# Top-32 attention followed by a gated feed-forward: token blocks of 256 in the feed-forward, other buffer counts, and the split first in GpSimd's order

## The chip, the cores and the metric

The kernel runs on one core of a Trainium2 chip. The core has five engines that each work through their own instructions in order: TensorE (matrix multiply; PE in the profile, PEld its weight loads), VectorE (DVE), ScalarE (ACT), GpSimd (POOL) and SyncE (SP, here only a queue of DMA issues). They meet at semaphores. The metric is the time of one execution on the device, in microseconds (us). The kernel before takes 1498.96 us, the median of three runs (1487.91, 1498.96, 1499.81).

## The reference

Attention for 8 batches x 8 heads, 576 tokens of 64 dimensions each. In every row of scores only the 32 largest survive. The result, 4608 tokens x 512, goes through a feed-forward of width 2048 with the activation h cos(h):

```python
scores = scale * np.matmul(q, k.transpose(0, 1, 3, 2))       # scale = 1/8
kth = np.partition(scores, -32, axis=-1)[..., -32:-31]
scores = np.where(scores >= kth, scores, -1e9)
scores = scores - np.max(scores, axis=-1, keepdims=True)
attn = np.exp(scores)
attn = attn / (np.sum(attn, axis=-1, keepdims=True) + 1e-09)
attn_out = np.matmul(attn, v)                                # 8, 8, 576, 64
x = attn_out.transpose(0, 2, 1, 3).reshape(4608, 512)
h = x @ w_in                                                 # 4608, 2048
return (h * np.cos(h)) @ w_out                               # 4608, 512
```

All in fp32, but the two weight matrices arrive as float64 and are turned into fp32 on the chip ("decoded").

## The kernel before

**Units and slots.** Tokens are cut into 36 tiles of 128. A unit is one tile and one pair of heads: 144 units, four to a tile. The main loop (line 815) has one slot for each unit, and a slot holds work for several units at once: VectorE finds the 32 largest of unit i (`topk_first`, `topk_round`), ScalarE masks and exponentiates unit i-1 (`bounds`, `mask`, `exponentials`), GpSimd splits unit i-2 into 16-bit halves that go out to DRAM and come back transposed (`send`: `split`, `write_halves`, `transposes`), and in even slots TensorE multiplies units i-4 and i-3 with v (`values`), after which ScalarE copies the product to xT (`take_values`) and VectorE scales it (`scale_values`). The scores of units i+1 and i+2 are mostly made in even slots too (`scores`), and ScalarE copies those of unit i+1 from PSUM to an SBUF tile s in slot i (`take_scores`, line 231). The first nine units and the last four take a shorter way (`early_slot`, `last_slot`). The order in each engine's queue is simply the order in which these functions are called.

**The search.** To halve VectorE's work, a row of 576 is folded: `rest` holds the larger of each two elements (VectorE, line 242) and `low` the smaller, which GpSimd makes as their sum (`fold_sum`, line 252) less the larger (`fold_low`, line 261). VectorE searches `rest` in four rounds, and then `low` in two. The reciprocal of a row's sum (line 362) is the first instruction of a slot on VectorE.

**The feed-forward** is cut into pieces that fill TensorE between the attention's matmuls. It works on blocks of tokens, here of 128. An ff1 piece (`ff1`, line 481) multiplies a block with some columns of w_in; two pieces fill one PSUM bank of 512 columns. When a bank is full, ScalarE reads it twice (`take_first`, lines 511 and 513), and two banks make a chunk of 1024 columns, held in a tile g. A chunk then goes through a range reduction in two steps (GpSimd, lines 533 and 542), a sine (ScalarE, line 552) and the product with h (`gate`, GpSimd, line 559). An ff2 piece (`ff2`, line 562) multiplies two of the 16 parts of a gated block with w_out; eight pieces fill one bank with 128 tokens x 512 outputs, which ScalarE copies out (`take_second`, line 582). In the profile one ff1 piece is 16 records of line 497, one ff2 piece four records of line 572, and each piece takes about 1.75 us of TensorE.

**What sets the order of pieces.** `feed` (line 606) is called three times a slot and spends a credit that grows by 5 less 0.9 for each unit scored (line 817). It prefers two pieces of a kind in turn; where the kind that is due isn't possible it takes the other, and where neither is, it stops. ff1 is possible once all units of a block are through (`can_first`), the weights are there, and fewer than `CHUNKS` chunks (with weights still being decoded, which share the tiles) are live; ff2 once the parts it reads have been gated for three calls of `feed` (`can_second`). Chunks are given back when the whole block has left through ff2. ff1 and ff2 share two PSUM banks (tag "mm", lines 491 and 566): a new bank can be written once ScalarE has read the one before in it. Where in ScalarE's order a full bank is read is set by the calls of `take_banks` in `slot` (lines 721, 741 and 758).

Of the kernel before, what the change touches and what calls it, by code (L numbers as in the profile page):

```python
# [10 lines left out]
F32 = mybir.dt.float32  # L11
# [6 lines left out]
P = 128  # L18
# [12 lines left out]
def kernel(  # L31
# [9 lines left out]
    nc = tc.nc  # L41
    ctx.enter_context(tc.manual_schedule())
    B, H, D, S = qT.shape
# [4 lines left out]
    NP = H // 2  # L48
# [8 lines left out]
    work = ctx.enter_context(tc.tile_pool(name="work", bufs=2))  # L57
# [28 lines left out]
    for i in range(DF // CW):  # L86
        w = consts.tile([P, NC, CW], F32, tag=f"w_in{i}", name=f"w_in{i}")
# [4 lines left out]
    for f in range(NF):  # L92
        w = consts.tile([P, DM], F32, tag=f"w_out{f}", name=f"w_out{f}")
        w_out.append(w)
        chunks.append((moe_w_out[f * P : (f + 1) * P, :], w))
    CHUNKS, XB = 7, 4
    ff = {"live": 0, "tick": 0, "now": 0, "credit": 0.0, "end": False, "kind": 0, "half": 0, "open": 0}

    wq = {"next": 0, "loaded": deque(), "second": deque(), "third": deque(), "done": 0, "ready": 0}
# [36 lines left out]
    def decode_second(n):  # L136

        for _ in range(min(n, len(wq["second"]))):
            st, w = wq["second"].popleft()
            wi = w.bitcast(I32)  # L140
            nc.vector.tensor_scalar(
                out=wi, in0=wi, scalar1=3, scalar2=None, op0=ALU.logical_shift_left
            )
            wq["third"].append((st, w))
# [14 lines left out]
    for t0 in range(0, B * S, P):  # L159
        parts = []  # L160
        for i, a in enumerate((t0, t0 + TAIL)):
            b, q0 = a // S, a % S
# [51 lines left out]
    room = [rim[:, j, 2 * (S - SB) :] for j in range(2)]  # L214
# [14 lines left out]
                    )  # L229

    def take_scores(u):
        s = u["s"] = work.tile([P, 2, S], F32, tag="s", name="s", bufs=4)
        nc.scalar.copy(out=s[:, :, 0:SB], in_=u["sc"][:, :, 0:SB])  # L233
        nc.scalar.copy(out=s[:, :, SB:S], in_=sc_ends[u["n"] % 2])  # L234
        if not u["folds"]:
            del u["sc"]
# [19 lines left out]
    def fold_low(u):  # L256

        if not u["folds"]:
            return
        low = u["low"].bitcast(I32)  # L260
        nc.gpsimd.tensor_tensor(  # L261
            out=low, in0=low, in1=u["rest"][:, :, HS:S].bitcast(I32), op=ALU.subtract
        )
# [9 lines left out]
    def topk_first(u, w):  # L273

        u["top"] = tops[u["n"] % len(tops)]
        merges = w and w["folds"]
        if merges:
            merge_first(w)
        if u["folds"]:
            fold_sum(u)  # L280
            fold_high(u)
            if u["n"] <= EARLY:
                fold_low(u)
        else:
            u["rest"] = work.tile([P, 2, S], F32, tag="rest", name="rest", bufs=1)
        if merges:
            merge_second(w)
        topk_round(u, 0)
# [52 lines left out]
    def mask(u):  # L341

        s, nb = u["s"], u.pop("nb")
        for j in range(2):
            nc.scalar.activation(  # L345
                out=s[:, j], in_=s[:, j], func=AF.Prelu, bias=nb[:, j, 1:2], scale=SCALE, alpha=FAR
            )
# [12 lines left out]
    def reciprocal(u):  # L360
        u["rden"] = small.tile([P, 2], F32, tag="rden", name="rden")
        nc.vector.reciprocal(u["rden"], u.pop("den"))
# [11 lines left out]
    def split(u):  # L374


        s = u.pop("s").rearrange("p j k -> p (j k)").bitcast(U16)
        halves = work.tile([P, 2, 2 * S + P], U16, tag="halves", name="halves", bufs=1)
        nc.gpsimd.tensor_copy(out=halves[:, :, 0 : 2 * S], in_=s.rearrange("p (k h) -> p h k", h=2))  # L379
        rden = u.pop("rden").bitcast(U16).rearrange("p (j h) -> p h j", h=2)  # L380
        nc.gpsimd.tensor_copy(
            out=halves[:, :, 2 * S :].rearrange("p h (j d) -> p h j d", j=2),
            in_=rden.unsqueeze(3).to_broadcast([P, 2, 2, D]),
        )
        u["halves"] = halves

    def write_halves(u):
        rows = u["rows"] = dram.tile([P, 2, 2 * S + P], U16, tag="rows", name="rows")
        nc.sync.dma_start(out=rows, in_=u.pop("halves"))

    def transposes(u):
        rows = u.pop("rows").rearrange("q h k -> (q h) k")
        pT = u["pT"] = work.tile([P, 2 * NT + 2, P], F32, tag="pT", name="pT", bufs=3)
        words = pT.rearrange("p c q -> p (c q)").bitcast(U16)
        nc.sync.dma_start_transpose(
            out=words.rearrange("p (c q) -> p c q", c=2 * NT + 2), in_=rows
        )
# [36 lines left out]
    def take_values(us):  # L434
        blk, hp, n = block_of[us[0]["tok"]], us[0]["hp"], len(us)
        if "xT" not in blk:
            blk["xT"] = work.tile([P, NP, P], F32, tag="xT", name="xT", bufs=5)
        to = blk["xT"][:, hp : hp + n].rearrange("p h q -> p (h q)")
        nc.scalar.copy(out=to, in_=room[0][:, 0 : n * P])
        for u in us:  # L440
            if not u["paired"]:
                del u["pT"]
        blk["left"] -= n
        blk["tick"] = ff["tick"]


    def scale_values(us):

        for u in us:
            to = block_of[u["tok"]]["xT"][:, u["hp"]]  # L450
            nc.vector.tensor_tensor(out=to, in0=to, in1=u.pop("pT")[:, 2 * NT + 1], op=ALU.mult)  # L451

    widths = [P] * (B * S // P)
    blocks, block_of = [], {}
    t0 = 0
    for w in widths:
        blk = {"t0": t0, "w": w, "left": 0, "g": [], "gated": []}
# [17 lines left out]
    def open_bank():  # L475

        if ff["open"] + len(full) == 2:
            take_banks()
        ff["open"] += 1

    def ff1(blk, i):
        w = blk["w"]
        nf = 256 // w
        part = i % 4
        if part == 0:
            blk["g"].append(ffw.tile([P, 1024], F32, tag="g", name="g", bufs=CHUNKS))
            blk["x"] = ffw.tile([P, 1024], F32, tag="x", name="x", bufs=XB)
            ff["live"] += 1
        if part % 2 == 0:
            open_bank()  # L490
            blk["mm"] = ps.tile([P, 512], F32, tag="mm", name="mm", bufs=2)
        g, mm = blk["g"][-1], blk["mm"]
        for a in range(nf):
            f = i * nf + a
            at = (part % 2 * nf + a) * w
            for c in range(NC):
                nc.tensor.matmul(  # L497
                    mm[:, at : at + w],
                    w_in[f // FC][:, c, (f % FC) * P : (f % FC + 1) * P],
                    blk["xT"][:, c],  # L500
                    start=c == 0,
                    stop=c == NC - 1,
                )
        if part % 2 == 0:
            return
        ff["open"] -= 1
        full.append((take_first, blk, g, blk["x"], mm, part // 2))
# [11 lines left out]
    def take_banks():  # L519
        while full:  # L520
            take, *what = full.popleft()
            take(*what)
# [177 lines left out]
    def send(x):  # L700

        split(x)
        write_halves(x)
        transposes(x)

    def slot(i, u, w, x, z):
        if x:
            reciprocal(x)
        if u:
            topk_first(u, w)  # L710
            decode_second(2)
        if x:
            send(x)
        if u:
            fold_low(u)
            topk_round(u, 1)
            topk_round(u, 2)
            topk_round(u, 3)
        made = scored.get(i, [])
        if z:  # L720
            take_banks()
        feed(1)

        ahead = i < EARLY + 5 * NP
        if z and not ahead:
            values(z)
        for m in made:
            scores(m)
        if z and ahead:
            values(z)  # L730


        late = len(made) > 0

        decoding = i < EARLY + 8
        if i % 2 and not decoding:
            sines(1)
        if w:
            bounds(w)
            mask(w)  # L740
        take_banks()
        if w and late:
            exponentials(w)
        if z and not ahead:
            take_values(z)
        take_scores(units[i + 1])
        if z and ahead:
            take_values(z)
        if z:
            scale_values(z)  # L750
        if w and not late:
            exponentials(w)
        load_weights(2)
        for load, b, hp in at_slot.get(i, []):
            load(b, hp)
        gate(1)
        feed(1 if len(made) == 2 else 2)
        take_banks()
        decode_third()
        decode_first(2)  # L760
        reduce_first()
        reduce_second()
        feed(1 if len(made) == 2 else 3)
        if decoding or i == LAST:
            sines(1)
# [49 lines left out]
    for i in range(NU + 1):  # L815
# [4 lines left out]
        u, w = (units[i - n] if 0 <= i - n < NU else None for n in range(2))  # L820
        x = units[i - 2] if EARLY <= i - 2 < LAST else None
# [54 lines left out]
```

## Time and profile before

| | TensorE | VectorE | ScalarE | GpSimd |
|---|---|---|---|---|
| busy, us | 1409.2 | 1332.0 | 1217.2 | 1165.1 |
| share of the span of 1491.0 us | 95% | 89% | 82% | 78% |

| group of instructions | count | mean ns of one |
|---|---|---|
| ff1 matmul, 128x128, line 497 | 4608 | 276 |
| ff2 matmul, 128x512, line 572 | 1152 | 603 |
| split, line 379 | 132 | 2107 |
| gate and second step of the reduction, lines 559 and 542 | 68 each | 2363, 2365 |
| sum and difference for `low`, lines 252 and 261 | 142 each | 1439, 1417 |
| ScalarE's two reads of an ff1 bank, lines 511 and 513 | 144 each | 588, 678 |
| ScalarE's copy of the scores, line 233 | 144 | 901 |

Every matmul of the program stands in the trace as two records. A record's length [...]overlaps the next record: 32 records of line 497 in a row take 3.57 us from the first start to the next group's start, so about 112 ns each, not 276. Rates are therefore read from start to start. VectorE's last search ends at 1422 us, TensorE's last matmul at about 1487 us: what lies between is feed-forward that is left over when attention is through.

### The profile page before, as it was taken

What the parts mean: (1) busy time and instruction counts of PE and PEld (TensorE: products, weight loads), DVE (VectorE), ACT (ScalarE), POOL (GpSimd) and SP (SyncE); (2) the same over time, 40 slices, a digit from 0 to 9 for tenths busy, and PEclk for the clock granted to TensorE, in tenths of its full rate; (3) what the DMA queues carried; (4) which work ended last, traced back from release to release, by engine and by line L of the source; (5) the groups of instructions that cost most, each with busy time, mean ns of one, the idle gap of its engine ahead of it and who ended that gap; (6) DMA issues with size and microseconds to landing.
All of it is one profiled execution on the core that took longest, in us unless ns stands there. A gap on an engine that the chain in (4) does not pass through costs nothing.

```text
span 1491.0 us, 30595 instructions
## 1 busy us (share of the span) xinstructions
PE 1409.2 (95%) x10360; PEld 1013.3 (68%) x10360; DVE 1332.0 (89%) x4764; ACT 1217.2 (82%) x2438; POOL 1165.1 (78%) x822
## 2 busy tenths in 40 slices
PE   5678599999999999999999999999999999999998
PEld 3456366777777777777767777677667777777665
DVE  6888899999999999999999999999999999999721
ACT  6887778888888888888888888888888888888651
POOL 5688777888888888888888888888888888888410
PEclk9888799999999999999999999999999999999999
DMA  8523476656665566556655566656765566555200
GB/s 265 159 86 101 138 203 160 156 146 187 190 165 149 149 176 192 160 151 193 180 165 149 149 179 175 171 149 160 198 170 146 149 165 181 160 147 148 70 8 15
DMA packets 405549, 229.54 MB, mean 154 GB/s; under 512 B 355088, under 2 KB 371728, under 8 KB 405392
## 3 DMA queue, kind: packets, MB, share of 16 engines
q1 hardware_dynamic: 399984, 217.93, 53.8%
q10 hardware_dynamic: 5408, 9.65, 1.8%
q8 instruction: 82, 1.34, 0.4%
q14 instruction: 75, 0.61, 0.1%
HBM read 45.09 MB, written 95.94 MB: 95 GB/s over the span
## 4 chain that ended last, share of the span: by engine, by line
PE 76%; ACT 12%; DVE 5%; DMA 4%; issue 1%; POOL 0%; SPq 0%; ACTq 0%; POOLq 0%
PE mm L497 29%; PE o L572 28%; PE rim L432 10%; PE sc L223 7%; DMA pT<-rows 2%; ACT s L353 2%; DVE top L323 2%; PE rim L223 2%; ACT s L345 2%; ACT s L233 1%; DVE rest L326 1%; ACT L353 1%; ACT L552 1%; ACT x L552 1%; DVE xT L451 1%
## 5 line engine op out<-in xcount | busy, mean ns | idle before, releaser
L497 PEld LDWEIGHTS mm<-xT,w_in 128*128 128x128 f32 x4608 | 538.2, 192 | 74.5 <-issue 51.4
L572 PE MATMUL o<-w_out,g 128*128 128x512 f32 x1152 | 540.4, 603 | 17.2 <-POOL w_out L151 13.6
L497 PE MATMUL mm<-xT,w_in 128*128 128x128 f32 x4608 | 542.1, 276 | 6.2 <-DVE xT L451 2.8
L323 DVE MAX8 top<-rest 128x8 f32<-128x288 f32 x1148 | 470.3, 451 | 0.0
L326 DVE MATCH_REPLACE8 rest<-top,rest 128x288 f32<-128x288 f32 (+1 forms) x860 | 376.3, 445 | 0.0
L252 POOL TENSOR_TENSOR low<-s 128x576 int32<-128x576 int32 x142 | 204.4, 1439 | 197.5 <-DVE top L323 81.1
L572 PEld LDWEIGHTS o<-w_out,g 128*128 128x128 f32 x1152 | 203.1, 191 | 205.0 <-issue 181.3
L379 POOL COPY halves<-s 128x2304 uint16<-128x2304 uint16 x132 | 278.1, 2107 | 0.5 <-DMA rows<-halves 0.5
L353 ACT ACTIVATE s<-s,nd 128x576 f32<-128x576 f32 x288 | 220.3, 766 | 14.0 <-ACT ob L582 13.2
L323 DVE MAX8 top<-low 128x8 f32<-128x288 f32 x568 | 229.1, 445 | 0.0
L345 ACT ACTIVATE s<-s,nb 128x576 f32<-128x576 f32 x288 | 205.3, 760 | 0.0
L261 POOL TENSOR_TENSOR low<-low,rest 128x576 int32<-128x576 int32 x142 | 201.2, 1417 | 1.8 <-DVE top L316 0.9
L432 PEld LDWEIGHTS rim<-pT,v 128*64 128x64 f32 x2560 | 135.0, 141 | 66.3 <-ACT nb L333 43.2
L432 PE MATMUL rim<-pT,v 128*64 128x128 f32 (+1 forms) x2560 | 163.9, 273 | 16.4 <-ACT pT L413 8.4
L511 ACT ACTIVATE g<-mm 128x512 f32<-128x512 f32 x144 | 84.6, 588 | 114.5 <-PE mm L497 114.5
L559 POOL TENSOR_TENSOR g<-g,x 128x1024 f32<-128x1024 f32 x68 | 160.7, 2363 | 8.2 <-ACT x L552 8.2
L542 POOL TENSOR_TENSOR x<-g,x 128x1024 f32<-128x1024 f32 x68 | 160.8, 2365 | 5.7
L223 PE MATMUL sc<-k,q 64*128 64x448 f32 (+1 forms) x640 | 155.0, 594 | 7.5 <-DVE rest L326 5.5
L233 ACT COPY s<-sc 128x896 f32<-128x896 f32 x144 | 129.8, 901 | 3.2 <-PE sc L223 3.2
L326 DVE MATCH_REPLACE8 low<-top,low 128x288 f32<-128x288 f32 x284 | 123.5, 441 | 0.0
L242 DVE TENSOR_TENSOR rest<-sc,s 128x576 f32<-128x576 f32 x142 | 106.1, 747 | 11.4 <-ACT s L234 11.4
L223 PEld LDWEIGHTS rim<-k,q 64*128 64x128 f32 (+1 forms) x640 | 59.6, 184 | 56.7 <-issue 53.4
(56 smaller groups left out, 1394.3 us busy)
## 6 DMA issues: line engine op xcount, KB each, us to landing
rows<-halves SPq DMA_DIRECT2D x132, 640.0 KB, 3.0
out_dram<-ob ACTq DMA_DIRECT2D x36, 256.0 KB, 2.1
q<-in_q_dram SPq DMA_DIRECT2D x31, 288.0 KB, 3.5
st<-in_moe_w_in_dram SPq DMA_DIRECT2D x16, 512.0 KB, 5.7
v<-in_v_dram SPq DMA_DIRECT2D x32, 256.0 KB, 3.1
st<-in_moe_w_out_dram SPq DMA_DIRECT2D x16, 512.0 KB, 4.1
k<-in_k_dram SPq DMA_DIRECT2D x31, 144.0 KB, 3.7
k<-in_k_dram SPq DMA_DIRECT2D x32, 128.0 KB, 3.6
```

The source lines that it names most:

```text
L223: nc.tensor.matmul(to[r0 : r0 + rows, j, 0 : k1 - k0], st["q"][d, q0 : q0 + rows], st["k"][d, k0:k1], start=True, stop=True,)
L252: nc.gpsimd.tensor_tensor(out=u["low"].bitcast(I32), in0=s[:, :, 0:HS], in1=s[:, :, HS:S], op=ALU.add)
L261: nc.gpsimd.tensor_tensor(out=low, in0=low, in1=u["rest"][:, :, HS:S].bitcast(I32), op=ALU.subtract)
L323: nc.vector.max(to[:, j], src[:, j])
L326: nc.vector.match_replace(rest[:, j], to[:, j], src[:, j], NEG)
L345: nc.scalar.activation(out=s[:, j], in_=s[:, j], func=AF.Prelu, bias=nb[:, j, 1:2], scale=SCALE, alpha=FAR)
L353: nc.scalar.activation(out=s[:, j], in_=s[:, j], func=AF.Exp, bias=nd[:, j : j + 1], scale=1.0, accum_out=den[:, j : j + 1],)
L379: nc.gpsimd.tensor_copy(out=halves[:, :, 0 : 2 * S], in_=s.rearrange("p (k h) -> p h k", h=2))
L432: nc.tensor.matmul(o[d, to], lhsT, rhs, start=c == 0, stop=c == NT)
L497: nc.tensor.matmul(mm[:, at : at + w], w_in[f // FC][:, c, (f % FC) * P : (f % FC + 1) * P], blk["xT"][:, c], start=c == 0, stop=c == NC - 1,)
L542: nc.gpsimd.tensor_tensor(out=x, in0=g, in1=x, op=ALU.subtract)
L572: nc.tensor.matmul(o, g[:, at : at + P], w_out[f], start=f == 0, stop=f == NF - 1)
```

## The change

The feed-forward's blocks hold 256 tokens, but for two of 128 at the start and two at the end. A block of 256 loads each part of w_in once for twice the tokens: ff1 has half the weight loads there, and matmuls of 256 columns. An ff1 piece is one part of w_in for 256 tokens in place of two parts for 128, two pieces still fill a bank and four a chunk; a block of 256 has 16 ff1 pieces, four chunks and 16 ff2 pieces. The tile xT holds 256 tokens, in three buffers in place of five of 128. To keep two such blocks live, `CHUNKS` goes from 7 to 8. To find the room in SBUF, s has three buffers in place of four; so that a new unit's scores don't wait for the split of an old one, `send` moves ahead of `topk_first` in `slot`, which puts the split ahead of the two folds in GpSimd's order.

```diff
-    CHUNKS, XB = 7, 4
+    CHUNKS, XB = 8, 4
...
-        s = u["s"] = work.tile([P, 2, S], F32, tag="s", name="s", bufs=4)
+        s = u["s"] = work.tile([P, 2, S], F32, tag="s", name="s", bufs=3)
...
-            blk["xT"] = work.tile([P, NP, P], F32, tag="xT", name="xT", bufs=5)
-        to = blk["xT"][:, hp : hp + n].rearrange("p h q -> p (h q)")
-        nc.scalar.copy(out=to, in_=room[0][:, 0 : n * P])
+            blk["xT"] = work.tile([P, NP, 2 * P], F32, tag="xT", name="xT", bufs=3)
+        q0 = us[0]["tok"] - blk["t0"]
+        to = blk["xT"][:, hp : hp + n, q0 : q0 + P]
+        nc.scalar.copy(out=to, in_=room[0][:, 0 : n * P].rearrange("p (h q) -> p h q", q=P))
...
-            to = block_of[u["tok"]]["xT"][:, u["hp"]]
+            blk = block_of[u["tok"]]
+            q0 = u["tok"] - blk["t0"]
+            to = blk["xT"][:, u["hp"], q0 : q0 + P]
...
-    widths = [P] * (B * S // P)
+    ends = 2
+    widths = [P] * ends + [2 * P] * ((B * S // P - 2 * ends) // 2) + [P] * ends
...
-                    blk["xT"][:, c],
+                    blk["xT"][:, c, 0:w],
...
         if x:
             reciprocal(x)
+            send(x)
         if u:
             topk_first(u, w)
             decode_second(2)
-        if x:
-            send(x)
```

## The prediction

> **What bounds the kernel now.** First the busy shares, then a long steady stretch, then TensorE's timeline over two slots, ScalarE's over the same slots, the waits, and the two ends.
>
> ```profile
> PE 1409.2 (95%) x10360; PEld 1013.3 (68%) x10360; DVE 1332.0 (89%) x4764; ACT 1217.2 (82%) x2438; POOL 1165.1 (78%) x822
> ```
> ```profile
> 340.00:1300.00 960.00, 952.07 (x7208) 687.98 (x7207) 909.48 (x3340) 826.54 (x1645) 814.57 (x556) 1.00 0.61 167
> ```
> The second line is one stretch: its length, then busy time of TensorE, its weight loads, VectorE, ScalarE and GpSimd. TensorE is busy 952 of 960 us, VectorE 909. TensorE leads, VectorE follows 4% behind.
>
> TensorE's timeline (start, length):
> ```profile
> 699.82 3.18 PE L497 MATMUL mm<-xT,w_in 128*128 128x128 f32 x27
> 702.83 3.60 PE L572 MATMUL o<-w_out,g 128*128 128x512 f32 x8
> 706.27 3.73 PE L497 MATMUL mm<-xT,w_in 128*128 128x128 f32 x32
> 709.84 1.88 PE L572 MATMUL o<-w_out,g 128*128 128x512 f32 x4
> ...
> 716.51 1.98 PE L572 MATMUL o<-w_out,g 128*128 128x512 f32 x4
> 718.33 3.73 PE L497 MATMUL mm<-xT,w_in 128*128 128x128 f32 x32
> ```
> The pattern repeats after 18.5 to 18.7 us (two slots). A pair of ff1 pieces (x32) always has ff2 pieces before the next pair. From start to start, 32 ff1 records take 3.57 us (112 ns each); 8 ff2 records take 3.44 us (429 ns each).
>
> ScalarE in the odd slot of that pair:
> ```profile
> 701.99 1.43 ACT L345 ACTIVATE s<-s,nb 128x576 f32<-128x576 f32 x2
> 703.32 0.58 ACT L511 ACTIVATE g<-mm 128x512 f32<-128x512 f32 x1
> 703.80 0.67 ACT L513 ACTIVATE x<-mm,quarter 128x512 int32<-128x512 f32 x1
> 704.37 0.89 ACT L233 COPY s<-sc 128x896 f32<-128x896 f32 x1
> ...
> 708.51 0.30 ACT L358 ACTIVATE den<-den,eps 128x2 f32<-128x2 f32 x1
> 710.04 0.60 ACT L511 ACTIVATE g<-mm 128x512 f32<-128x512 f32 x1 [1.24 <-PE mm L497]
> ```
> ScalarE empties an ff1 bank (L511, L513) at two places in a pair of slots: after the mask (703.32), and after the exponentials (710.04). Between them it is full. The bank that TensorE ended at 703.00 is free at 704.47, 1.47 us later.
>
> Waits:
> ```profile
> ACT g L511 <- PE mm L497: 114.5, 76, 5.8
> DVE rden L362 <- ACT den L358: 72.9, 67, 7.4
> PE o L572 <- POOL w_out L151: 13.6, 2, 9.8
> ```
> ScalarE waits for TensorE, VectorE for ScalarE; so TensorE sets the pace. Its only large wait is at the start, for the last decoded weights. One line near the end shows the wait that matters below, an ff1 pair that needs a bank ScalarE has not emptied:
> ```profile
> 1430.48 2.05 PE L497 MATMUL mm<-xT,w_in 128*128 128x128 f32 x16 [1.23 <-ACT x L513]
> ```
>
> **What the skill says.** The Trainium skill, "PSUM — Partial Sum Buffer", Specifications (TRN2): eight banks of 2 KiB per partition. This kernel has given all away: two to rim, four to sc, two to mm, which ff1 and ff2 share. "TensorE: Matmul & The Clock Gate", Architectural detail: ScalarE and VectorE are strictly first in, first out, TensorE only pulls weight loads ahead; the timelines agree, no matmul overtakes a waiting one. Same page, Back-to-back issue gap and LDWEIGHTS: a matmul costs its columns plus about 2.5 ns, a load of 128 columns about 107 ns. The trace agrees: 429 ns for 512 columns; 112 ns for 128, of which the stream alone would be (429 - 2.5)/4 + 2.5 = 109. "Perfetto Trace Analysis", Identifying Performance Opportunities: a gap that keeps repeating on the engine that should be full can mean too little PSUM for the next tile. The trace of before has no such gap in its steady part; I expect one to appear.
>
> **The change, part by part.**
>
> *256 columns in ff1.* For 32 of the 36 token tiles two records of 112 ns become one of (429 - 2.5)/2 + 2.5 = 216 ns: 8 ns saved for each of 4608 x 32/36 / 2 = 2048 records. **-16 us**. Bounds: 0, if 256 columns cost twice 112; -21, at 427/2 ns. ScalarE's and GpSimd's work in the feed-forward is the same in number and size; ff2 also.
>
> *Order of the pieces.* I stepped the rules of lines 589 to 623 slot by slot, by count alone (0 is an ff1 piece, 1 an ff2 piece; the bar is where the next slot begins). For before this gives the order of the timeline, ff1 and ff2 in turn. After repeats every 8 slots:
> ```
> before, slots 40-47:  110|01100|110|01100|110|01100|110|01100
> after,  slots 40-47:  110|01111|110|00000|110|01100|110|01100
> ```
> A block of 256 has four chunks, and ff2 of its first token half needs all four while they are still being made, so ff2 runs dry once a block and five ff1 pieces come in a row, with an ff2 bank open (6 of its 8 pieces done). Then ff1 has one bank alone: each of the two next pairs has to wait until ScalarE has emptied the pair before. On the odd slot above: a bank is full at 703.00 and free at 704.47; the next pair takes 3.45 us and is full at about 708; ScalarE's place for it is after the exponentials, which end at 708.81, plus 1.27 us for the two reads, 710.08. The third pair starts at about 710.1; with no wait it would have started at 702.84 + 3.45 = 706.3. **3.8 us of TensorE idle per block.** Behind the waiting matmul stand ff2, the values and the scores of the even slot (711.65 to 716.5 before); behind those ScalarE's copy of the scores, then VectorE's next unit. GpSimd is held too: the chunk's range reduction and all after it come 3.5 us late. These run side by side and add once. Counted: 13 such slots (35, 43, ... 131), and two with one wait of about 1.5 us (33, 139): 13 x 3.8 + 3 = **+52 us**. Floor: an idle ScalarE takes 1.21 us from TensorE's modelled end (the median of the other bank) and the end is modelled 0.16 late, so some 1.4 us a wait, 28 waits, 39 us. VectorE's slack (0.74 us before the reciprocal at 708.84) can't win it back: TensorE is the late one, and it is full in the slots that follow.
>
> *Start and tail.* A block of 256 waits for eight units, not four. By the same count ff1 and ff2 are short of pieces in slots 13 to 18, 23 to 25 and 33; at slot 36 the feed-forward is 19 pieces behind before, and stays so: 46 pieces remain after the last unit, 27 before. Tail: 19 x 1.73 us = +33. Against it: the starved slots shrink from TensorE's pace to VectorE's (8.73 and 9.13 us by the reciprocals), and with eight chunks the last weight is loaded a slot earlier (slot 11 for 12), which takes some 9 of the 13.6 us of w_out waiting. Slots 12 to 18 took 79.6 us; seven at VectorE's pace plus 4 us of waiting are 66.5: -13. Slots 19 to 35: about -4. Together **+16 us** (0 to +25).
>
> *xT in three of 256.* Six tiles of room for five; ff1 reads a block about 3.5 tiles behind attention by the count: no wait. The strided copies have the same elements: 0.
>
> *Three score buffers.* ScalarE's copy of a new unit's scores waits for GpSimd's split of the unit three before. The copy starts 1.7 us (odd) or 4.8 us (even) after that split ends (medians of before): hidden, and split first only widens it.
>
> *Split first on GpSimd.* The sum and difference for the low half move behind 2.5 us of split and broadcast. The difference ends 1.3 (odd) and 1.8 us (even) ahead of VectorE's search of it. In odd slots GpSimd is idle 0.9 us beforehand, so little is lost. In even slots the gate (2.36) and both reductions (3.42) now fall into the odd slot before, GpSimd's split starts about 1.6 us late and the difference ends some 0.6 us too late: VectorE waits 0.6 us per pair, within its 0.74 us of slack. 0; at worst +25 (0.6 in some 42 pairs).
>
> Sum: 1499 - 16 + 52 + 16 = **1551 us**.
>
> **The rivals.** *A, waits at half price:* ScalarE comes to the full banks sooner, since it has fewer reads in the slots before, and the start breaks even: 1499 - 16 + 26 + 5 = 1514. For: the floor above; against: ScalarE is busy without a gap from 699.03 to 708.8. *B, faster:* five ff1 in a row cost nothing because TensorE has run ahead or the bank is released early, and start and tail cancel: 1499 - 16 = 1483. For: ScalarE and VectorE wait 187 us today; against: TensorE, not they, is full, and the line at 1430.48 shows the wait already. *C, GpSimd becomes a second limit:* its burst in odd slots is not absorbed: 1551 + 25 = 1576. For: 0.6 of 0.74 us is thin; against: 78% busy.
>
> **How the numbers follow.** The main case 0.62, A 0.17, B 0.12, C 0.09. Range 1505 to 1578: it takes in A and C and the bounds of start and tail, and leaves out B. Faster by over 1%: 0.10 (most of B); within 1%: 0.06 (the rest of B, the weak end of A); slower: 0.84.
>
> **What would show it.** ff1 records of 128x256, start to start 216 ns. TensorE waiting on ScalarE's second read of mm some 28 times, 1.4 to 2.2 us each, every 8 slots. Slots of 9.5 us with one longer by 3.8. VectorE's last search no earlier than at 1422 us plus 30; a tail of about 46 pieces. ScalarE's score copies not waiting on GpSimd. Wrong if the matmul after a full bank starts at once, or if VectorE's waits grow through the low difference instead.

## The result, and the profile after

The changed kernel takes 1583.74 us (median of four, 1583.35 to 1585.12), against 1497.63 us before (median of four): a ratio of 1.059, 95% interval 1.054 to 1.064. It is slower, as forecast, but by 86 us where 52 were forecast, and 6 us outside the range.

First the busy shares of the changed kernel, then the stretch from the start of slot 36 to that of slot 132 (length, then busy time of TensorE, weight loads, VectorE, ScalarE, GpSimd), before and after, then five waits of the changed kernel over its whole length (total, times, longest):

```profile
PE 1424.4 (90%) x8312; PEld 950.0 (60%) x8312; DVE 1337.0 (85%) x4767; ACT 1212.0 (77%) x2432; POOL 1161.9 (73%) x818
```
```profile
389.50:1299.50 910.00, 903.08 (x6866) 652.18 (x6866) 862.82 (x3168) 783.14 (x1561) 773.39 (x529) 1.00 0.61 166
394.50:1354.80 960.30, 904.65 (x5328) 598.57 (x5328) 865.86 (x3169) 785.37 (x1561) 778.37 (x528) 1.00 0.58 157
```
```profile
POOL x L537 <- ACT x L517: 82.2, 36, 6.3
DVE top L323 <- POOL low L261: 55.8, 18, 4.4
PE mm L501 <- ACT x L517: 51.7, 32, 4.0
PE mm L501 <- DVE xT L454: 13.9, 12, 3.7
PE o L576 <- POOL w_out L151: 2.9, 1, 2.9
```

No engine is full any more: the same 96 slots took 910.0 us before with 903 us of TensorE busy, now 960.3 us with 905. Of the waits, the third is the one that was forecast, TensorE's for a full bank; the first two, GpSimd waiting for the same bank and VectorE for GpSimd's `low`, are new as well and not in the list of before.

The time can be laid out by VectorE's reciprocals, the first instruction of each slot:

| | before | after | difference | forecast |
|---|---|---|---|---|
| up to slot 36 | 389.5 | 394.5 | +5 | -14 (start -17, waits in slots 33 and 35 +5.3, 288 records of -8 ns) |
| slots 36 to 132 | 910.0 | 960.3 | +50 | +33 (12 blocks of +3.8, 1536 records of -8 ns) |
| slot 132 to the end of ScalarE's last copy | 188.4 | 223.8 | +35 | +33 (tail +33, wait in slot 139 +1.5, 224 records of -8 ns) |

The forecast column is the sum of the prediction, cut at the same places. The two profiled executions lie 91 us apart, a little more than the medians, because the one of before took 1492.8 us.

One burst, TensorE's timeline of the changed kernel:

```profile
626.18 2.86 PE L501 MATMUL mm<-xT,w_in 128*128 128x256 f32 x12 [1.39 <-DVE xT L454]
630.48 3.72 PE L501 MATMUL mm<-xT,w_in 128*128 128x256 f32 x16 [1.44 <-ACT x L517]
635.87 3.72 PE L501 MATMUL mm<-xT,w_in 128*128 128x256 f32 x16 [1.68 <-ACT x L517]
639.43 1.88 PE L576 MATMUL o<-w_out,g 128*128 128x512 f32 x4
```

ScalarE in the same slot:

```profile
629.75 0.67 ACT L517 ACTIVATE x<-mm,quarter 128x512 int32<-128x512 f32 x1
...
634.46 0.29 ACT L358 ACTIVATE den<-den,eps 128x2 f32<-128x2 f32 x1
634.66 0.58 ACT L515 ACTIVATE g<-mm 128x512 f32<-128x512 f32 x1
635.14 0.68 ACT L517 ACTIVATE x<-mm,quarter 128x512 int32<-128x512 f32 x1
```

The pair of ff1 pieces at 630.48 starts when ScalarE ends its second read at 630.42, the pair at 635.87 when it ends the next at 635.82, behind the exponentials: the two waits of the prediction, at the two places it named. There is a third ahead of them, 1.39 us for VectorE's scaling of xT: the new block's first piece has run four records and needs the block's last two units, which VectorE scales only after its search of low (from 625.86). And GpSimd, in the same slots:

```profile
635.90 1.04 POOL L537 TENSOR_SCALAR x<-x 128x1024 f32<-128x1024 int32 x1 [3.86 <-ACT x L517]
637.03 2.36 POOL L546 TENSOR_TENSOR x<-g,x 128x1024 f32<-128x1024 f32 x1
639.34 2.09 POOL L379 COPY halves<-s 128x2304 uint16<-128x2304 uint16 x1
641.38 0.39 POOL L381 COPY halves<-rden 128x256 uint16<-128x256 uint16 x1
641.75 1.41 POOL L252 TENSOR_TENSOR low<-s 128x576 int32<-128x576 int32 x1
643.24 1.40 POOL L261 TENSOR_TENSOR low<-low,rest 128x576 int32<-128x576 int32 x1
```

The reduction waits for the late bank; the split, the sum and the difference queue behind it, and VectorE's search of low starts at 644.67 after 3.10 us of waiting.

From start to start, ff1 matmuls in slots 36 to 132 took 388.2 us of TensorE; 1536 records of 216 ns, which is what 128x256 records in a row cost, would be 331.8. So 56.4 us, 4.7 in each of the 12 blocks, are waits. Before, 3072 records took 342.8 us.

### The profile page after: what moved, and what is told of

It is laid out like the page before. It is cut to its first block, busy times and chain, and to the rows that moved or that the text cites. A ratio compares the mean times of both kernels' runs of the same rounds, so it can differ in the third digit from the quotient of the medians.

```text
span 1581.7 us, 26463 instructions
## 1 busy us (share of the span) xinstructions
PE 1424.4 (90%) x8312; PEld 950.0 (60%) x8312; DVE 1337.0 (85%) x4767; ACT 1212.0 (77%) x2432; POOL 1161.9 (73%) x818
## 4 chain that ended last, share of the span: by engine, by line
PE 46%; ACT 26%; DVE 15%; DMA 5%; POOL 5%; issue 2%; SPq 1%; ACTq 0%; POOLq 0%
PE o L576 17%; PE mm L501 15%; PE rim L432 7%; DVE top L323 6%; PE sc L223 5%; ACT s L353 4%; DVE rest L326 4%; ACT s L345 4%; DMA pT<-rows 3%; ACT L353 3%; ACT s L233 2%; ACT L556 2%; ACT x L517 2%; ACT x L556 2%; DVE rest L242 2%
## 5 line engine op out<-in xcount | busy, mean ns | idle before, releaser
L501 PE MATMUL mm<-xT,w_in 128*128 128x256 f32 (+1 forms) x2560 | 537.7, 364 | 65.6 <-ACT x L517 51.7
L501 PEld LDWEIGHTS mm<-xT,w_in 128*128 128x128 f32 x2560 | 449.3, 192 | 181.7 <-ACT x L517 70.3
L576 PEld LDWEIGHTS o<-w_out,g 128*128 128x128 f32 x1152 | 214.6, 192 | 229.8 <-issue 196.8
L323 DVE MAX8 top<-low 128x8 f32<-128x288 f32 x568 | 229.9, 447 | 55.8 <-POOL low L261 55.8
L252 POOL TENSOR_TENSOR low<-s 128x576 int32<-128x576 int32 x142 | 200.7, 1414 | 12.2 <-DVE top L323 6.6
L223 PE MATMUL sc<-k,q 64*128 64x448 f32 (+1 forms) x640 | 161.9, 611 | 23.3 <-DMA k<-in_k_dram 19.7
L563 POOL TENSOR_TENSOR g<-g,x 128x1024 f32<-128x1024 f32 x66 | 156.3, 2368 | 17.2 <-ACT x L556 17.2
L537 POOL TENSOR_SCALAR x<-x 128x1024 f32<-128x1024 int32 x67 | 70.5, 1052 | 87.5 <-ACT x L517 82.2
```

Source lines behind the costliest of these rows:

```text
L223: nc.tensor.matmul(to[r0 : r0 + rows, j, 0 : k1 - k0], st["q"][d, q0 : q0 + rows], st["k"][d, k0:k1], start=True, stop=True,)
L252: nc.gpsimd.tensor_tensor(out=u["low"].bitcast(I32), in0=s[:, :, 0:HS], in1=s[:, :, HS:S], op=ALU.add)
L323: nc.vector.max(to[:, j], src[:, j])
L501: nc.tensor.matmul(mm[:, at : at + w], w_in[f // FC][:, c, (f % FC) * P : (f % FC + 1) * P], blk["xT"][:, c, 0:w], start=c == 0, stop=c == ...
L576: nc.tensor.matmul(o, g[:, at : at + P], w_out[f], start=f == 0, stop=f == NF - 1)
```

## The experiments

Times are medians of two to twelve runs; each group is compared with runs of the kernel before on the same chip (1493 to 1495 us; 1497.6 for the changed kernel). "Slots" are 36 to 132. The last three columns come from one profiled execution of each kernel. The times of all128_old alone spread over 15 us (1487.5 to 1502.1), so differences of a few us in these columns say little.

| kernel | us | ratio to before (95%) | slot 36 at | slots | after slot 132 |
|---|---|---|---|---|---|
| before | 1493-1495 | 1 | 389.5 | 910.0 | 188.4 |
| after | 1583.7 | 1.059 (1.054-1.064) | 394.5 | 960.3 | 223.8 |
| all128 | 1517.4 | 1.016 (1.014-1.017) | 387.7 | 935.0 | 187.7 |
| all128_old | 1495.3 | 1.001 (0.998-1.003) | 391.1 | 915.4 | 184.4 |
| all128_psum | 1474.0 | 0.988 (0.986-0.990) | 381.3 | 901.5 | 184.4 |
| old_order | 1612.3 | 1.078 (1.076-1.081) | 401.1 | 981.6 | 223.9 |
| lag1 | 1619.4 | 1.083 (1.081-1.085) | 410.9 | 976.7 | 225.5 |
| lag2 | 1659.0 | 1.110 (1.107-1.112) | 409.8 | 1011.7 | 230.0 |
| no_burst | 1571.0 | 1.051 (1.046-1.055) | 394.4 | 942.8 | 224.2 |
| no_burst_old | 1549.7 | 1.036 (1.033-1.040) | 396.4 | 923.9 | 223.0 |
| burst_in_before | 1561.5 | 1.044 (1.040-1.048) | 389.8 | 970.5 | 193.5 |
| ends16_old | 1539.6 | 1.030 (1.028-1.033) | 392.3 | 929.2 | 215.4 |
| reduce_early | 1564.0 | 1.048 (1.045-1.050) | 382.8 | 952.9 | 221.3 |
| wide_fixed | 1507.0 | 1.009 (1.007-1.011) | 380.9 | 900.7 | 222.4 |
| before_psum | 1488.5 | 0.996 (0.995-0.997) | 384.3 | 912.1 | 186.7 |
| direct128 | 1472.9 | 0.986 (0.983-0.989) | 379.9 | 900.1 | 184.4 |

**all128: everything but the wide blocks.**

```diff
-    ends = 2
+    ends = 18
```

> The changed kernel with blocks of 128 throughout: eight chunks, three score buffers, the wide xT tile and the split first are kept. Theory (the blocks of 256 cost the time, by bank waits of about 4.7 us a block and 19 pieces put off to the tail): 1490 to 1500 us, no TensorE wait on ScalarE's reads of mm in the steady part, 26 pieces left after attention. Rival (the split first and three score buffers make GpSimd late, VectorE waits for the low difference): 1530 us or more, with VectorE's wait for low still above 30 us.

Measured 1517 us: between the two. The wide blocks are most of the loss, but 22 us come without them, and VectorE hardly waits for low (once, 3.6 us). What it does instead, VectorE's and then GpSimd's timeline of this kernel:

```profile
648.57 0.81 DVE L323 MAX8 top<-low 128x8 f32<-128x288 f32 x2
649.30 1.90 DVE L454 TENSOR_TENSOR xT<-xT,pT 128x128 f32<-128x128 f32 x2
651.12 0.15 DVE L362 RECIPROCAL rden<-den 128x2 f32<-128x2 f32 x1
```
```profile
648.74 2.11 POOL L379 COPY halves<-s 128x2304 uint16<-128x2304 uint16 x1
```

Two scalings of xT, 0.28 us each elsewhere, take 1.90 us and end just after GpSimd's split. With the split first, GpSimd begins it before the slot does, as soon as the exponentials are done, and that is when VectorE scales. 63 of 132 scalings took over 500 ns (before: 6). The time of a held instruction counts as busy, so no wait shows it. The Trainium skill, "SBUF — State Buffer", section "SBUF: two separate sides", says that VectorE and GpSimd share a port pair, which one instruction holds for its whole length, and that a VectorE instruction with two SBUF inputs needs it against a GpSimd one that reads SBUF. The prediction had not looked at that; all128_old and all128_psum test it.

**old_order: the split back behind the folds in the changed kernel.**

```diff
         if x:
             reciprocal(x)
-            send(x)
         if u:
             topk_first(u, w)
             decode_second(2)
+        if x:
+            send(x)
         if u:
```

> The changed kernel with the split back behind the folds in GpSimd's order, three score buffers kept. Theory: 1584 us within 10, since TensorE's bank waits stay. Rival (the order costs the time): 1545 us or less.

Measured 1612 us, 28 more: neither. Where there are bursts, the split first is a help. Why isn't settled; TensorE waits 18.2 us in twelve places for a unit's transposed halves here, 5.0 in three in the changed kernel (both in the steady part).

**lag1 and lag2: ff2 allowed sooner after the gate.**

```diff
-        lag = 3 if 3 * NP < ff["now"] < NU - NP else 2
+        lag = 1 if 3 * NP < ff["now"] < NU - NP else 2
```

> The changed kernel with ff2 allowed one call of feed after the gate in the long middle part, in place of three. By count ff1 and ff2 then alternate in twos and only 7 pairs of ff1 follow a full bank (28 before), all but one before slot 32; 46 pieces are still left after attention. Theory: bank waits fall from 52 us to about 10, the low wait goes with them, and some 10 to 15 us of waiting for the gate come in their place: 1530 to 1555 us, the tail unchanged. Rival (GpSimd's order): 1575 us or more.

> The changed kernel with ff2 allowed two calls of feed after the gate. By count one pair of ff1 per block follows a full bank in place of two. Theory, if TensorE's bank waits decide: 12 blocks by some 1.7 to 2.5 us are won, 1555 to 1565 us. If instead the chunk's late reduction on GpSimd decides (it stays, since the bank is still read after the exponentials): 1575 us or more.

Both missed the range of the theory by far, 1619 and 1659 us, and fell where the rivals had put them (1575 or more). lag1 has no bursts in the steady part, but two other waits instead: TensorE for the gate, and 47 held scalings (76.5 us). In lag2 the order is shifted so that in nearly every pair of slots the chunk's second bank is the late one; by the waits GpSimd's reduction then decides, the second branch of its expectation. The waits of lag1 (first line) and lag2, between 390 and 1350 us:

```profile
PE o L576 <- POOL g L563: 40.9, 13, 8.4
```
```profile
POOL x L537 <- ACT x L517: 167.1, 45, 6.3
DVE top L323 <- POOL low L261: 120.8, 45, 3.4
```

So removing bursts by moving ff2 tells nothing clean. The next four runs take the wide blocks, the bursts and the split's place apart.

**all128_old: blocks of 128 and the split behind the folds** (both edits above).

> The changed kernel with blocks of 128 throughout and the split back behind the folds; eight chunks, three score buffers and the wide xT tile stay. Theory (the 22 us that the run with blocks of 128 lost are VectorE's scaling of xT held up by GpSimd's split, which now starts before the slot does: 63 of 132 scalings took over 500 ns, 109 us in all): 1489 to 1502 us, fewer than ten long scalings. Rival (three score buffers or eight chunks cost it): 1510 us or more.

Measured 1495.3 us, ratio 1.001, four long scalings. Eight chunks, three score buffers and the wide xT tile together cost nothing; the order alone cost the 22 us.

**no_burst: a rule that ends the bursts.** `n2` counts ff2 pieces, `last` is 1 when the last piece filled an ff1 bank; the lines that keep them are left out here.

```diff
...
+        if i % 2 == 0 and ff["tick"] % 3 == 0 and ff["n2"] % 8 and ff["last"]:
+            return False
         return i % 4 > 0 or ff["live"] + staged() < CHUNKS
...
```

> The changed kernel with one rule added to feed: in the last call of a slot no ff1 piece opens a bank right behind a filled one while an ff2 bank is open. By count all 28 cases but two go, ff1 and ff2 alternate in twos, 48 pieces are left after attention (46 before). Theory (two causes, bank waits in the bursts, and scalings held up by the split where there is no burst): the bank waits fall below 10 us, the long scalings come up as in the run with blocks of 128, slots 36 to 132 take about 935 us in place of 960, 1550 to 1565 us. Rival (bank waits are not what the bursts cost): 1580 us or more. Rival (bank waits alone): 1535 us or less.

Measured 1571 us, above the range. The slots shrank by 17.5 us to 942.8, not by 25, and long scalings came up to 56 (96 us) in place of 8 (12.6 us). Waits for ScalarE's second read did not all go either: 16.5 us of them are left between 390 and 1350 us, where under 10 were expected.

**no_burst_old: the same, and the split behind the folds.**

> The same rule, and the split back behind the folds. Theory: neither bank waits nor held scalings; slots 36 to 132 at TensorE's pace, 885 to 910 us; 1510 to 1535 us, what is left above the kernel before being the start and the tail. Rival: 1560 us or more.

Measured 1550 us, better than all wide versions so far, but above the range: the slots took 923.9 us. A possible reason, read from one slot: a bank of ff2 now ends where ScalarE copies it out in its full odd slot (in slot 61, 11.73 us long, a copy and 0.45 us of waiting for it stand ahead of the sine). With these runs the two factors make a table of the slots' time:

| slots 36 to 132, us | split behind the folds | split first |
|---|---|---|
| blocks of 128 | 915.4 | 935.0 |
| blocks of 256, no bursts | 923.9 | 942.8 |
| blocks of 256, bursts | 981.6 | 960.3 |

The bursts cost 58 us in twelve blocks (4.8 each) with the old order, and 17.5 with the new. Of the 40 us between, 19 are held scalings, which the new order pays without bursts and hardly with them; the rest is the open question of old_order.

**burst_in_before: bursts forced on the kernel before.**

```diff
-            for kind in (ff["kind"], 1 - ff["kind"]):
+            due = {3: 0, 5: 1}.get((ff["now"] - 1) % 8) if 36 < ff["now"] < 137 else None
+            due = ff["kind"] if due is None else due
+            for kind in (due, 1 - due):
```

> The kernel before, blocks of 128 and all else as it was, but every eight slots five ff1 pieces in a row are forced, and five ff2 pieces two slots later. By count 28 pairs of ff1 then follow a full bank with an ff2 bank open, as in the changed kernel, and 30 pieces are left after attention in place of 27. Theory: 13 bursts by some 4 us and 5 us of tail, 1545 to 1565 us, with some 28 TensorE waits on ScalarE's second read of mm. Rival (the bursts cost nothing by themselves, the wide blocks do): 1510 us or less.

Measured 1561.5 us, inside the range. Part of the edit is not a burst of ff1: five ff2 pieces in a row follow two slots later. The bank wait of this kernel, over the whole run:

```profile
PE mm L497 <- ACT x L513: 42.1, 29, 1.6
```

Blocks of 128, old order, old buffers, and the slots grow by 60.5 us: 5.0 a burst. The order of the pieces is a cause by itself, without any wide block.

**all128_psum: blocks of 128 (`ends = 18`) and split first, but the scaling reads SBUF once.**

```diff
-        for u in us:
+        for k, u in enumerate(us):
...
-            nc.vector.tensor_tensor(out=to, in0=to, in1=u.pop("pT")[:, 2 * NT + 1], op=ALU.mult)
+            nc.vector.tensor_tensor(
+                out=to, in0=room[0][:, k * P : (k + 1) * P], in1=u.pop("pT")[:, 2 * NT + 1],
+                op=ALU.mult,
+            )
```

> The changed kernel with blocks of 128 throughout and the split first, but VectorE's scaling of xT takes its first operand from PSUM, where the product still lies, so that it reads SBUF once; ScalarE's copy is kept. Theory (two reads of SBUF are what GpSimd's split holds up): no scaling near 2 us in the steady part, 1488 to 1502 us, as with the split behind the folds. Rival (the later sum and difference for low cost the 22 us): 1512 us or more.

No scaling took over 293 ns:

```profile
652.80 0.49 DVE L454 TENSOR_TENSOR xT<-rim,pT 128x128 f32<-128x128 f32 x2
```

And the time fell to 1474.0 us, below the expected range and below the kernel before by 1.2%. The held scaling is shown: the long times are there with two operands in SBUF and gone with one in PSUM, at the same place in the order. The split first is a gain once it collides with nothing; before_psum below says how much of the 1.2% is its own.

**ends16_old: only two blocks of 256** (`ends = 16`, split behind the folds).

> The changed kernel with the split behind the folds and only two blocks of 256, in the middle of 32 of 128. By count feed runs dry in slots 69 to 81 about, 18 more pieces are left after attention (44), four pairs of ff1 follow a full bank. Theory (one step from 128 to 256 puts off 18 pieces for good, whatever follows): 1495 + 18 x 1.73 + 4 x 2.2 less some 8 us that the dry slots are shorter, 1515 to 1535 us, and the time after slot 132 up by 31 us. Rival (the tail grows with the number of wide blocks): 1497 to 1507 us.

Measured 1539.6 us, 5 above the range and 44 above all128_old; 31 us of it after slot 132 (215.4 against 184.4), as expected for 18 put-off pieces. The changed kernel with its 16 wide blocks stands at 223.8, so one step to wide blocks pays most of the tail. The 14 us more in the slots, where about 1 was expected, were not followed up.

**reduce_early: the reduction ahead of the second call of feed.**

```diff
         gate(1)
+        reduce_first()
+        reduce_second()
         feed(1 if len(made) == 2 else 2)
...
         decode_first(2)
-        reduce_first()
-        reduce_second()
```

> The changed kernel with the two steps of the range reduction issued ahead of the second call of feed, so that GpSimd never waits in a burst for the bank that ScalarE reads after the exponentials. Theory (TensorE's bank waits decide, GpSimd's lateness lies beside them): slots 36 to 132 within 12 us of 960, 1570 to 1590 us. Rival (GpSimd's late reduction, and through it the low difference, decides): VectorE's waits for low gone and 1550 us or less.

Measured 1564 us, below the range of the theory and above the rival's. VectorE's waits for low are gone, TensorE's for ScalarE's second read stay (46.1 us, 28 times). The slots took 952.9, 7 less, so in the steady part GpSimd's lateness lies mostly beside TensorE's waits, as expected. But slot 36 begins at 382.8, 12 us sooner: at the start it does not.

**wide_fixed, direct128, before_psum.** The first has the rule of no_burst, the scaling from PSUM and the early reduction; the second is all128_psum without ScalarE's copy where the scaling reads PSUM; the third is the kernel before with the scaling from PSUM. The edit that only the second has:

```diff
-        nc.scalar.copy(out=to, in_=room[0][:, 0 : n * P].rearrange("p (h q) -> p h q", q=P))
+        if not us[0]["paired"]:
+            nc.scalar.copy(out=to, in_=room[0][:, 0 : n * P].rearrange("p (h q) -> p h q", q=P))
```

> The changed kernel, blocks of 256 kept, with all three waits taken away: the rule of feed that ends the bursts, the scaling of xT from PSUM, and the range reduction ahead of the second call of feed. Theory (what is left is the tail of put-off pieces, 48 after attention, against 16 us of faster ff1 records): slot 36 at about 383, slots 36 to 132 in 885 to 905 us, after slot 132 some 220 us (188 before); 1495 to 1520 us in all. Rival (the waits were all of it, the wide blocks win once they are gone): 1475 us or less.

> Blocks of 128, split first, eight chunks, three score buffers, the scaling of xT from PSUM, and ScalarE's copy of the product left out where the scaling reads PSUM itself (66 copies of 0.37 us). TensorE sets the pace, ScalarE only follows, so little is won: 1466 to 1478 us, against 1474 with the copy. If ScalarE's chain to the denominators sets the slots of 9.3 and 9.4 us: 1455 us or less. If VectorE's later release of the PSUM bank holds the next values up: 1480 us or more.

> The kernel before with the scaling of xT from PSUM alone; blocks of 128, four score buffers, seven chunks and the split behind the folds stay. Six of its 132 scalings were held up, 10 us in all. Theory (the split first wins some 20 us by itself once it doesn't collide): 1485 to 1497 us. Rival (reading PSUM is what wins, the split first gives nothing): 1470 to 1480 us.

All three fell into the first range. wide_fixed against all128_psum (which lacks the early reduction): the start alike (380.9 and 381.3), the slots alike (900.7 and 901.5), 38 us more after slot 132. So with the waits gone the wide blocks still lose, by the tail alone, and their faster records (338.9 us of ff1 in place of 342.8) show almost nowhere. before_psum, at 0.996 of before, says that reading PSUM by itself wins 0.4%; the other 0.8% of all128_psum, some 12 us, come with the split first. Leaving ScalarE's copy out wins nothing that can be told from zero, as expected if ScalarE only follows. direct128, at 0.986 of before, is the fastest here.

## Why the prediction was right in direction and too small

*256 columns in ff1, -16 us.* Right for the record: 216 ns, 2048 of them. What the Trainium skill gives at the place that the prediction cites ("TensorE: Matmul & The Clock Gate", Back-to-back issue gap) is 216 ns for an isolated matmul of 512 columns, half of the 429 that a record takes here; so the estimate rested on the trace's 429 and took from the page only the form, columns plus 2.5 ns. That TensorE's saved time shortens the kernel isn't shown: in wide_fixed some 8 of the 338.9 us of ff1 are waits again, and its slots are as long as with blocks of 128.

*Bursts, +52 us.* The mechanism was right in each part: the count of pieces, the two waits, their places in ScalarE's order, 32 waits of 1.6 us. burst_in_before shows that it is a cause. The size was 4.7 us a block in place of 3.8, since a third wait, for the scaling of the block's last units, was not foreseen (12 waits, 13.9 us). That makes 11 of the 17 us that the forecast was short in slots 36 to 132; the other 6 were not placed. What I expected around it was wrong: between bursts the slots don't stay at 9.5 us, they run mostly at VectorE's 8.73 and 9.13, and two long ones follow the burst (12.40 and 11.17 in slots 60 and 61). The eight slots 60 to 67 took 75.0 us before and 78.3 after.

*Start and tail, +16 us: the step that failed, in its start.* The tail was right: +33 forecast, +35 measured, and the put-off pieces are what it is. By count 26 pieces are left after attention with blocks of 128 (all128 and its variants), 44 in ends16_old and 48 in wide_fixed; 18 and 22 pieces more, at the prediction's 1.73 us, are 31 and 38 us, and 31 and 38 were measured. The start was forecast at -17, which with the first bank waits and the shorter records makes -14 up to slot 36; it came out at +5. For slots 12 to 18, 79.0 us before by the reciprocals, "seven at VectorE's pace plus 4 us of waiting are 66.5", but they took 75.0. TensorE's wait for w_out did fall, from 13.6 to 2.9 us, but slot 12 still took 18.70 us (18.87 before): ScalarE's queue set it, not TensorE. ScalarE stood 4.70 us for a weight. The sine, two reads, the mask, the exponentials and the copies came behind, and at the end two scalings of xT that met GpSimd's split (from 162.64) and took 2.98 us:

```profile
150.60 0.69 ACT L130 ACTIVATE w_out<-st 128x512 f32<-128x512 f32 x1 [4.70 <-DMA st<-in_moe_w_out_dram]
151.17 0.71 ACT L133 ACTIVATE st<-st 128x512 int32<-128x512 uint32 x1
151.89 1.28 ACT L556 ACT_TABLE_LOAD   x1
153.18 1.15 ACT L556 ACTIVATE x<-x,halfpi 128x1024 f32<-128x1024 f32 x1
...
161.97 2.98 DVE L454 TENSOR_TENSOR xT<-xT,pT 128x128 f32<-128x128 f32 x2 [4.04 <-ACT xT L440]
```

Slot 18, now nearly free of feed-forward, waited 5.9 us for k instead and took 11.73 us (15.20 before). Slots 19 to 35, forecast at "about -4" and some 5 us of first bank waits, measured +12: once a wide block was there, five, three and five ff1 pieces came in three slots, their banks were read late, and the reduction, the split and low with them; reduce_early takes 10.5 us of that away. I had counted which pieces were missing and not what runs when all come at once. Nor does the gain of the starved slots show once the waits are gone: slot 36 begins at 380.9 us in wide_fixed and at 381.3 with blocks of 128 in all128_psum.

By places the forecast was short by 19 us up to slot 36, 17 in the slots and 3 after slot 132 in the profiled executions, 39 in all; by the medians the kernel is 33 above the forecast 1551.

*Three score buffers, eight chunks, xT: 0.* Right, taken together (all128_old).

*Split first: 0, at worst +25.* Wrong in its reason. It asked whether low is late and not what the earlier split meets. By itself the move costs 19 to 20 us in the slots, through held scalings that no wait shows; in the changed kernel, with its bursts, it gains 21.

*Rivals.* B is refuted: burst_in_before. A is refuted: the waits came at the full price, and the start did not pay for the tail. C, GpSimd as a second limit, was given too little: VectorE waited 55.8 us for low in the changed kernel (none in the list before), which the prediction had named as a sign of being wrong. Most of it lies beside TensorE's waits, but the early reduction, which does away with it, makes the kernel some 20 us faster, 12 of them at the start.

What stays open: why no_burst_old needs 924 us for its slots and not 900 was read from one slot, not tried. Why bursts cost more with the old order, and why the split first wins some 12 us once it collides with nothing, wasn't followed. lag1 mixes gate waits and held scalings, and they weren't separated.

## What to carry to other kernels

Before making a block larger, step the order of work through by count, and look for places where one kind of piece runs several times in a row: two buffers that suffice for alternating work don't for a run of one kind, and the wait is as long as the distance to the next place where the reader's queue empties a buffer. Where an engine is starved, the slots shrink only to the next engine's pace, and the work put off is paid in full at the end; which queue really sets a slot has to be read there, not taken from the longest wait. When an instruction moves on GpSimd, check what VectorE then runs beside it with two SBUF inputs.

## What the runs showed of the hardware

A VectorE product of two SBUF tiles of 128x128, 0.28 us alone, took up to 2.18 us when GpSimd's 2.11 us copy ran, and stands as busy in the profile; with one operand in PSUM the longest was 0.29 us. A matmul record of 128x256 fp32 repeats every 216 ns, one of 128x128 every 112 ns, one of 128x512 every 429 ns. In slot 12 of the changed kernel, after 2.89 us of waiting, 20 records of ff2 took 11.85 us, where 8.6 would do at 429 ns: they came every 853 ns up to 164.2 us and every 429 ns from there, and the granted clock was 0.50 between 158 and 164 us and 0.99 between 164 and 170.
